# Attention with beacon keys followed by an ELU feed-forward layer: moving the ELU's second half from VectorE to ScalarE, and issuing the attention casts whole

## The chip, the cores and the metric

The kernel runs on one core of one Trainium2 chip. The metric is the device time of one execution in microseconds. The profiled span is 1.6 to 1.9 us shorter than the device time, because the profile counts from the first to the last instruction.

Engine names: PE is TensorE (matrix multiply; PEld is its weight load), DVE is VectorE, ACT is ScalarE, POOL is GpSimd, SP is SyncE. "Two-input" means an elementwise instruction that reads two tensors.

## The reference, cut to what matters

```python
# attention over 8 batches, 8 heads, 576 queries, 16 beacon keys in front of 576 causal keys, D = 64
scores = scale * np.matmul(q, k_all.transpose(0, 1, 3, 2))
scores = np.where(causal, -1e9, scores)
a = np.exp(scores - scores.max(-1, keepdims=True)); a /= a.sum(-1, keepdims=True) + 1e-09
x = (a @ v_all)                            # -> 4608 tokens x 512
# feed-forward
h = x @ w_in                               # 512 -> 2048
g = np.where(h > 0.0, h, np.exp(np.minimum(h, 0.0)) - 1.0)      # ELU
return g @ w_out                           # 2048 -> 512
```

## The kernel before

The program is one hand-ordered list of steps. The list fixes the order of each engine's own instructions, and in the timelines below DVE takes its instructions in that order: at one place of the changed kernel it sat idle for 0.54 us while the inputs of `M` became ready, and still ran the two instructions emitted ahead of `M` first. The 4608 tokens are cut into output tiles of 512 (the first one into two halves, numbered 0 and 1). A **stage** is one tile of the feed-forward layer together with one attention batch: stages 2 to 7 have both, stages 8 and 9 have no attention left. A stage has 16 **chunks**; a chunk is one block of 128 hidden units for 512 tokens, and between its own matmuls it carries a slice of the previous tile's output projection and of the attention.

The steps that the argument touches:

```python
@step
def F(t, i):     # PE: hidden matmul, four 128-deep matmuls into PSUM bank hps (two such banks)
@step
def e(t, i):     # ACT: e = exp(h), PSUM -> SBUF fp32
    eb[t, i] = melt.tile([P, 512], FP32, tag="e", bufs=2, name="e")
    nc.scalar.activation(out=eb[t, i], in_=flat(hp[t, i]), func=AFT.Exp, bias=0.0, scale=1.0)
@step
def r(t, i):     # DVE: r = min(e, 1) - 1, SBUF -> SBUF
    rb[t, i] = melt.tile([P, 512], FP16, tag="r", name="r")
    nc.vector.tensor_scalar(
        out=rb[t, i], in0=eb[t, i], scalar1=1.0, scalar2=1.0, op0=ALU.min, op1=ALU.subtract)
@step
def g(t, i):     # DVE: g = max(h, r); reads PSUM, so it is what frees the hps bank
    ...
    nc.vector.tensor_tensor(out=gh[k][:, i % UN, :], in0=flat(hp[t, i]), in1=rb[t, i], op=ALU.max)
```

`S` is a score matmul (into one of the PSUM banks that scores, row sums and attention outputs share), `x` its Exp on ACT, `m` the causal mask product on DVE. `L` and `W` are the matmuls for row sums and attention output, `n` the reciprocal on ACT, and `M` the product on DVE that writes the attention output into `xT` and thereby frees its PSUM bank. `Q` and `J` are the output projection and its eviction; it uses Strassen's scheme, for which `Z` makes sums of `gt` on DVE and `wt` makes sums of the weights, once.

The attention inputs of later batches are cast from fp32 to bf16 by DMAs that POOL issues. Before, each cast of q or k is cut into four pieces (the five loads of the values are issued one by one), and in front of each, from tile 2 on, POOL makes a one-element copy of the newest hidden chunk (a **gate**), so that the issue falls at a known place relative to DVE's work (in front of the 57 gates POOL waited 70.3 us in sum for DVE's `gt`):

```python
def gated():
    if last[0] is not None and last[0][0] >= 2:
        nc.gpsimd.tensor_copy(out=gate, in_=gh[...][0:1, last[0][1] % UN, 0:1])
@step
def kq(b, c):                        # one of 8 pieces: two heads of q or of k
    ...
    gated()
    nc.gpsimd.dma_start(out=scr[b, n_][:, hs, :], in_=(q, k)[n_][b, hs].rearrange("h s d -> s h d"))
```

The softmax here doesn't subtract the row's maximum and nothing guards it: scores larger than these inputs give would overflow.

## Time and profile before

The median was 359.14 us in three runs (358.25 to 359.36).

| | before |
|---|---|
| profiled span | 356.5 us |
| PE, DVE, ACT, POOL busy | 95%, 81%, 65%, 38% |
| stages 2 to 8, start to start | 33.37, 39.71, 37.81, 37.56, 36.67, 35.56, 26.37 us |

Stage lengths here and below are computed from the trace as the time from the first hidden matmul of a stage to that of the next. (The prediction writes 39.1 us for stage 3; the trace gives 39.71, and the prediction's 3.0 us above stage 6 fits that figure.) The busy line of the profile page, and the start of its chain (the work that ended last, followed back), of the kernel before:

```profile
PE 339.9 (95%) x4331; PEld 209.3 (59%) x4331; DVE 290.5 (81%) x655; ACT 233.4 (65%) x363; POOL 136.1 (38%) x207
PE 63%; DVE 24%; ACT 8%; issue 3%; ACTq 0%; DVEq 0%
```

PE is the fullest engine, and a quarter of the chain runs through DVE. The groups of instructions of the same kernel (line, engine, operation, output<-inputs, count | busy us, mean ns of one | idle time of the engine just before them, and what ended it):

```profile
L438 PE MATMUL hps<-xT,w_in 128*128 128x512 f16 (+1 forms) x640 | 147.8, 359 | 5.6 <-DVE gt L462 5.4
L448 ACT ACTIVATE e<-hps 128x512 f32<-128x512 f32 x144 | 86.1, 599 | 54.3 <-PE hps L438 52.8
L462 DVE TENSOR_TENSOR gt<-hps,r 128x512 f16<-128x512 f32 x144 | 99.5, 691 | 6.1
L453 DVE TENSOR_SCALAR r<-e 128x512 f16<-128x512 f32 x144 | 72.2, 501 | 12.7 <-ACT e L448 11.1
L568 POOL COPY gate<-gt 1x1 f16<-1x1 f16 x57 | 18.5, 324 | 70.5 <-DVE gt L462 70.3
L583 POOL DMA_DIRECT2D scr<-in_q_dram x20 | 27.3, 1365 | 2.0 <-DMA w_out<-in_moe_w_out_dram 1.5
```

ELU takes two DVE passes, `r` (501 ns on average) and `g` (691 ns), 1.19 us of DVE per chunk, while ACT idles 54 us in front of its Exps. The mean of `r` hides two populations: the 91 that no POOL cast touches take 421 ns, and the 53 that stand beside a cast take 638 ns on average and up to 1.29 us. The waits of PE, with their totals, number and longest, in us:

```profile
PE hps L438 <- DVE gt L462: 5.4, 13, 0.8
PE sc L279 <- DVE xT L386: 2.3, 4, 0.9
PE sc L279 <- ACT et L289: 1.1, 3, 0.7
PE ut L316 <- issue: 1.0, 1, 1.0
```

The first line is the one the change aims at: PE wants the hidden bank, and DVE's `g` has not yet freed it. Here is one at the end of stage 4:

```profile
176.15 0.49 DVE L406 TENSOR_TENSOR xT<-ut,rl 128x128 f16<-128x128 f32 x2 [0.74 <-ACT rl L352]
...
177.10 0.69 DVE L462 TENSOR_TENSOR gt<-hps,r 128x512 f16<-128x512 f32 x1
...
177.84 1.02 PE L438 MATMUL hps<-xT,w_in 128*128 128x512 f16 x4 [0.52 <-DVE gt L462]
```

The `g` that frees the bank stood behind the last `M` of the stage (L406), which had itself waited for the reciprocal on ACT.

### The profile page before, as it was taken

The numbers are of one execution on the slowest core, as the hardware profiler recorded it, in microseconds if no ns is written. First come the engines' busy times: TensorE is split into PE (matmuls) and PEld (weight loads), VectorE is DVE, ScalarE is ACT, GpSimd is POOL, SyncE is SP. The second block draws the span as 40 slices with busy tenths as digits, with TensorE's granted clock in tenths as the row PEclk, the third lists the DMA queues.
The fourth block names the chain that finished last, engine by engine and source line by source line (L and its number), as shares of the span: only waits on it lengthen the run. The fifth ranks groups of instructions, "written<-read, shape, count | busy, mean of one in ns | idle before, by whom it ended". The sixth has DMA issues, their size and how long they took to land.

```text
span 356.5 us, 10381 instructions
## 1 busy us (share of the span) xinstructions
PE 339.9 (95%) x4331; PEld 209.3 (59%) x4331; DVE 290.5 (81%) x655; ACT 233.4 (65%) x363; POOL 136.1 (38%) x207
## 2 busy tenths in 40 slices
...
GB/s 121 159 191 185 180 204 145 122 174 80 127 94 112 102 107 73 155 104 99 63 163 104 95 94 110 152 5 31 61 32 2 31 59 32 29 61 30 31 88 90
DMA packets 127759, 34.76 MB, mean 98 GB/s; under 512 B 111328, under 2 KB 126176, under 8 KB 127712
## 3 DMA queue, kind: packets, MB, share of 16 engines
...
q10 hardware_dynamic: 576, 0.13, 0.2%
...
## 4 chain that ended last, share of the span: by engine, by line
PE 63%; DVE 24%; ACT 8%; issue 3%; ACTq 0%; DVEq 0%
PE hps L438 25%; PE ops L535 18%; DVE gt L462 6%; PE sc L279 5%; DVE r L453 5%; PE lt L316 5%; ACT et L289 3%; PE ops L471 3%; DVE xT L386 3%; DVE gt L492 3%; DVE osb L551 2%; PE ut L316 2%; PE w L206 2%; DVE et L305 2%; ACT rl L349 2%
## 5 line engine op out<-in xcount | busy, mean ns | idle before, releaser
L438 PE MATMUL hps<-xT,w_in 128*128 128x512 f16 (+1 forms) x640 | 147.8, 359 | 5.6 <-DVE gt L462 5.4
L448 ACT ACTIVATE e<-hps 128x512 f32<-128x512 f32 x144 | 86.1, 599 | 54.3 <-PE hps L438 52.8
L289 ACT ACTIVATE et<-sc 128x832 f16<-128x832 f32 x128 | 104.3, 871 | 16.3 <-PE sc L279 15.0
L462 DVE TENSOR_TENSOR gt<-hps,r 128x512 f16<-128x512 f32 x144 | 99.5, 691 | 6.1
L535 PEld LDWEIGHTS <-gt 128*128 128x128 f16 x768 | 75.2, 98 | 28.8
L438 PEld LDWEIGHTS <-w_in 128*128 128x128 f16 x640 | 56.7, 97 | 52.7 <-issue 13.5
L453 DVE TENSOR_SCALAR r<-e 128x512 f16<-128x512 f32 x144 | 72.2, 501 | 12.7 <-ACT e L448 11.1
L535 PE MATMUL ops<-wt,gt 128*128 128x256 f16 x384 | 52.5, 273 | 0.0
L535 PE MATMUL ops<-w_out,gt 128*128 128x256 f16 x384 | 51.4, 273 | 0.0
L305 DVE TENSOR_TENSOR et<-et,triu 128x256 f16<-128x256 f16 (+2 forms) x164 | 38.5, 268 | 13.7 <-ACT et L289 13.3
L568 POOL COPY gate<-gt 1x1 f16<-1x1 f16 x57 | 18.5, 324 | 70.5 <-DVE gt L462 70.3
L134 POOL DMA_DIRECT2D v<-in_v_dram x40 | 34.4, 865 | 7.8 <-issue 3.5
L492 DVE TENSOR_TENSOR gt<-gt 128x1024 f16<-128x1024 f16 x48 | 32.5, 681 | 0.0
L583 POOL DMA_DIRECT2D scr<-in_q_dram x20 | 27.3, 1365 | 2.0 <-DMA w_out<-in_moe_w_out_dram 1.5
L583 POOL DMA_DIRECT2D scr<-in_k_dram x20 | 27.2, 1361 | 1.2 <-DMA w_out<-in_moe_w_out_dram 1.2
L316 PEld LDWEIGHTS <-v 128*32 128x32 f16 x1248 | 20.7, 94 | 9.6 <-issue 3.5
L279 PE MATMUL sc<-qkd 64*128 64x208 bf16 (+5 forms) x320 | 22.3, 252 | 2.4 <-DVE xT L386 2.3
L551 DVE TENSOR_TENSOR osb<-ops,sm 128x512 f32<-128x512 f32 x24 | 16.4, 681 | 4.4 <-issue 3.4
L279 PEld LDWEIGHTS <-qkd 64*128 64x128 bf16 x320 | 11.2, 94 | 14.0 <-issue 9.3
L316 PE MATMUL ut<-et,v 128*32 128x64 f16 (+6 forms) x840 | 17.0, 225 | 1.4 <-issue 1.0
L544 ACT COPY sm<-ops 128x512 f32<-128x512 f32 x24 | 14.3, 595 | 5.3 <-PE ops L535 5.2
L535 PE MATMUL ops<-w_out,s 128*128 128x256 f16 x128 | 17.6, 273 | 0.0
...
## 6 DMA issues: line engine op xcount, KB each, us to landing
...
```

Source lines behind the costliest of these rows:

```text
L134: nc.gpsimd.dma_start(out=st[b][2][r0:r0 + n, j, :, :], in_=v[b, :, ilo[j]:ilo[j] + n, :].rearrange("h s d -> s h d"),)
L279: nc.tensor.matmul(out=s[:, h, a - c0:e - c0], lhsT=t[D * h:D * (h + 1), 1, P * j:P * (j + 1)], rhs=t[D * h:D * (h + 1), 0, NB + qa + a - ...
L289: nc.scalar.activation(out=ets[b, p][:, :, GW * g:GW * (g + 1)], in_=sc[b, p, g][:, :, 0:GW], func=AFT.Exp, bias=0.0, scale=SCALE)
L305: nc.vector.tensor_tensor(out=o, in0=o, in1=triu[0:kc[j], :, t0:t0 + e - a], op=ALU.mult)
L316: nc.tensor.matmul(out=t[32 * i:32 * (i + 1), a - qa:e - qa], lhsT=ones[0:kc[j], :] if half is None else v16[0:kc[j], j, h, 32 * half:32 * ...
L438: nc.tensor.matmul(out=h[:, n_, :], lhsT=w_in16[:, cc, P * fc:P * (fc + 1)], rhs=xt[k][:, cc, a - TT * k:e - TT * k], start=(cc == 0), sto ...
L448: nc.scalar.activation(out=eb[t, i], in_=flat(hp[t, i]), func=AFT.Exp, bias=0.0, scale=1.0)
L453: nc.vector.tensor_scalar(out=rb[t, i], in0=eb[t, i], scalar1=1.0, scalar2=1.0, op0=ALU.min, op1=ALU.subtract)
L462: nc.vector.tensor_tensor(out=gh[k][:, i % UN, :], in0=flat(hp[t, i]), in1=rb[t, i], op=ALU.max)
L492: nc.vector.tensor_tensor(out=o_, in0=a_, in1=b_, op=op_)
L535: nc.tensor.matmul(out=xy[t, n_][:, qd, :], lhsT=lw[:, P * qd:P * (qd + 1)], rhs=wt_[:, c, :], start=(first and qd == 0 and c == 0), stop= ...
L583: nc.gpsimd.dma_start(out=scr[b, n_][:, hs, :], in_=(q, k)[n_][b, hs].rearrange("h s d -> s h d"))
```

## The change

The intent: ELU(h) = min(exp(h) - 1, relu(h)). (For h > 0 exp(h) - 1 is the larger, for h < 0 relu is 0 and exp(h) - 1 is below it.) From the last four chunks of tile 1 on (132 of the 144 chunks of the kernel), both Exp and Relu leave PSUM on ACT, and DVE joins them in one pass that touches only SBUF. That gives DVE one pass per chunk in place of two, and the hidden PSUM bank is freed by ACT. With `r` gone from there on, the casts are no longer cut up nor gated. The diff, cut to its core:

```diff
     def e(t, i):
-        eb[t, i] = melt.tile([P, 512], FP32, tag="e", bufs=2, name="e")
+        eb[t, i] = melt.tile([P, 512], FP32, tag="e", bufs=3, name="e")
         nc.scalar.activation(out=eb[t, i], in_=flat(hp[t, i]), func=AFT.Exp, bias=0.0, scale=1.0)
+    @step
+    def u(t, i):
+        rb[t, i] = melt.tile([P, 512], FP16, tag="r", name="r")
+        nc.scalar.activation(out=rb[t, i], in_=flat(hp[t, i]), func=AFT.Relu, bias=0.0, scale=1.0)
+    @step
+    def kk(t, i):
+        nc.vector.scalar_tensor_tensor(
+            out=half(t, i), in0=eb[t, i], scalar=1.0, in1=rb[t, i], op0=ALU.subtract, op1=ALU.min)
+    op["k"] = kk
...
-    def gated():
-        if last[0] is not None and last[0][0] >= 2:
-            nc.gpsimd.tensor_copy(out=gate, in_=gh[...][0:1, last[0][1] % UN, 0:1])
...
-        gated()
-        hs = slice(2 * x_, 2 * x_ + 2)
-        nc.gpsimd.dma_start(out=scr[b, n_][:, hs, :], in_=(q, k)[n_][b, hs].rearrange("h s d -> s h d"))
+        t = scr[b, n_] = dram.tile([S, H, D], BF16, tag=f"scr{n_}", name="scr")
+        nc.gpsimd.dma_start(out=t[:, :, :], in_=(q, k)[n_][b].rearrange("h s d -> s h d"))
... (in the lists: r.t.i g.t.i become u.t.i k.t.i; lv.c.0 to lv.c.4 become lv.c; eight kq become lk.d.0 lk.d.1)
```

The order of PE's 4331 matrix multiplies is the same before and after.

More of the change, by code (lines that the diff above doesn't have):

```diff
@@ L446, in e, with half @@
     def e(t, i):
-        eb[t, i] = melt.tile([P, 512], FP32, tag="e", bufs=2, name="e")
+        eb[t, i] = melt.tile([P, 512], FP32, tag="e", bufs=3, name="e")
         nc.scalar.activation(out=eb[t, i], in_=flat(hp[t, i]), func=AFT.Exp, bias=0.0, scale=1.0)
+    @step
+    def u(t, i):
+        rb[t, i] = melt.tile([P, 512], FP16, tag="r", name="r")
+        nc.scalar.activation(out=rb[t, i], in_=flat(hp[t, i]), func=AFT.Relu, bias=0.0, scale=1.0)
+    def half(t, i):
+        k = t, i // UN
+        if k not in gh:
+            gh[k] = gpool.tile([P, UN, 512], FP16, tag="g", name="gt")
+        return gh[k][:, i % UN, :]
+    @step
[3 more added lines that the diff above has]
+    op["k"] = kk
     @step
@@ L457, in g @@
     def g(t, i):
-        k = t, i // UN
-        if k not in gh:
-            gh[k] = gpool.tile([P, UN, 512], FP16, tag="g", name="gt")
-        last[0] = t, i
-        nc.vector.tensor_tensor(out=gh[k][:, i % UN, :], in0=flat(hp[t, i]), in1=rb[t, i], op=ALU.max)
+        nc.vector.tensor_tensor(out=half(t, i), in0=flat(hp[t, i]), in1=rb[t, i], op=ALU.max)
     @step
@@ L561, with lk @@
     scr, qkd = {}, {}
-    last = [None]
-    gate = konst.tile([1, 1], FP16, name="gate")
-    def gated():
-        if last[0] is not None and last[0][0] >= 2:
-            nc.gpsimd.tensor_copy(out=gate, in_=gh[last[0][0], last[0][1] // UN][0:1, last[0][1] % UN, 0:1])
-    @step
-    def lk(b):
-        new_stage(b)
-        load_qk(b, 0, H)
-    @step
-    def kq(b, c):
-        x_, n_ = c // 2 % 2 + 2 * (c // 4), c % 2
-        if c < 2:
-            scr[b, n_] = dram.tile([S, H, D], BF16, tag=f"scr{n_}", name="scr")
-        gated()
-        hs = slice(2 * x_, 2 * x_ + 2)
-        nc.gpsimd.dma_start(
-            out=scr[b, n_][:, hs, :], in_=(q, k)[n_][b, hs].rearrange("h s d -> s h d"))
+    @step
+    def lk(b, n_=None):
+        if b < BD:
+            new_stage(b)
+            load_qk(b, 0, H)
+            return
+        t = scr[b, n_] = dram.tile([S, H, D], BF16, tag=f"scr{n_}", name="scr")
+        nc.gpsimd.dma_start(out=t[:, :, :], in_=(q, k)[n_][b].rearrange("h s d -> s h d"))
     @step
@@ L601, in lv @@
     @step
-    def lv(b, *js):
-        gated()
-        load_v(b, list(js) or list(range(NKC)))
+    def lv(b):
+        load_v(b, list(range(NKC)))
     def run(names):
@@ L613 @@
     run("""
-    warm.12 bt bk cb.0.0 cb.0.1 cb.0.3 cb.0.2 warm.3 T.0.0 ck.0.0 cq.0.0 warm.4.64 S.0.0.0 S.0.0.1
-    T.0.1 x.0.0.0 cq.0.1 m.0.0.0 x.0.0.1 S.0.0.2 warm.1.64 S.0.0.3 ck.0.1 x.0.0.2 cb.1.0 warm.1.64
-    T.0.2 S.0.1.0 x.0.0.3 x.0.1.0 warm.1.64 S.0.1.1 m.0.0.2 cq.0.2 x.0.1.1 warm.2.64 S.0.1.2
-    warm.2.64 T.0.3 wo.0 wo.1 lv.1 lk.2 wo.2 wo.3 m.0.0.3 x.0.1.2 S.0.1.3 ck.0.2 m.0.1.0 m.0.1.2
-    ck.0.3 warm.5.64 S.0.3.0 x.0.1.3 warm.2.64 S.0.2.0 cb.1.1 x.0.3.0 m.0.1.3 x.0.2.0 m.0.3.0
@@ L619 @@
-    warm.2.64 S.0.3.1 warm.2.64 S.0.2.1 x.0.3.1 m.0.2.0 x.0.2.1 warm.2.64 S.0.3.2 x.0.3.2 L.0.A
-    S.0.3.3 n.0.A x.0.3.3 cb.1.3 m.0.3.2 W.0.A.1 T.1.0 M.0.A.1 m.0.3.3 W.0.A.0 S.0.2.2 W.0.B.0.1
-    ck.1.0 M.0.A.0 x.0.2.2 S.0.2.3 cb.1.2 T.1.1 x.0.2.3 m.0.2.2 S.1.0.0 ck.1.1 m.0.2.3 F.0.0 e.0.0
-    r.0.0 F.0.3 x.1.0.0 g.0.0 m.1.0.0 W.0.B.1.1 e.0.3 S.1.0.1 S.1.1.0 x.1.0.1 F.0.2 r.0.3 x.1.1.0
-    e.0.2 g.0.3 L.0.B m.1.0.1 m.1.1.0 n.0.B S.1.1.1 F.0.1 r.0.2 g.0.2 F.0.5 M.0.B.0.1 M.0.B.1.1
-    x.1.1.1 S.1.1.2 S.1.0.2 W.0.B.0.0 m.1.1.1 e.0.1 r.0.1 x.1.1.2 e.0.5 W.0.B.1.0 lv.2 g.0.1 x.1.0.2
@@ L625 @@
-    M.0.B.0.0 S.1.0.3 F.0.7 x.1.0.3 e.0.7 cb.2.0 T.1.2 r.0.5 m.1.1.2 m.1.0.2 ck.1.2 T.1.3 g.0.5
-    m.1.0.3 r.0.7 F.0.4 ck.1.3 g.0.7 e.0.4 M.0.B.1.0 S.1.1.3 F.0.6 cb.2.1 x.1.1.3 G.0.0.0 r.0.4 kq.3.0
-    g.0.4 e.0.6 m.1.1.3 r.0.6 kq.3.1 S.1.3.0 S.1.3.1 x.1.3.1 g.0.6 F.1.1 m.1.3.1 e.1.1 x.1.3.0 G.0.1.0
-    F.1.0 r.1.1 kq.3.2 g.1.1 S.1.3.2 e.1.0 m.1.3.0 r.1.0 kq.3.3 x.1.3.2 S.1.2.0 x.1.2.0 F.1.2 G.0.0.1 g.1.0 e.1.2
-    S.1.3.3 S.1.2.1 m.1.3.2 F.1.5 m.1.2.0 x.1.3.3 cb.2.2 x.1.2.1 r.1.2 kq.3.4 S.1.2.2 e.1.5 g.1.2 F.1.3
@@ L630 @@
-    m.1.3.3 G.0.1.1 x.1.2.2 m.1.2.1 r.1.5 kq.3.5 e.1.3 g.1.5 m.1.2.2 S.1.2.3 r.1.3 kq.3.6 T.2.0 x.1.2.3 ck.2.0
-    g.1.3 F.1.6 F.1.7 S.2.0.0 S.2.0.1 e.1.6 x.2.0.0 x.2.0.1 G.0.0.2 S.2.0.2 m.1.2.3 x.2.0.2
-    G.0.1.2 T.2.1 r.1.6 kq.3.7 g.1.6 e.1.7 m.2.0.0 T.2.2 m.2.0.1 ck.2.1 m.2.0.2 G.0.0.3 ck.2.2 L.1.0 r.1.7
-    W.1.0.0 g.1.7 S.2.0.3 o.0.0 n.1.0 cb.2.3 F.1.4 M.1.0.0 x.2.0.3 e.1.4 m.2.0.3 G.0.1.3 r.1.4
-    W.1.0.1 o.0.1 L.1.1 M.1.0.1 g.1.4 W.1.1.0 n.1.1 W.1.1.1 M.1.1.0 R.1 S.2.1.0 M.1.1.1 x.2.1.0
@@ L635 @@
-    G.1.1.0 n.1.R m.2.1.0 M.1.R F.2.1 F.2.0 e.2.1 S.2.1.1 S.2.1.2 e.2.0 r.2.1 g.2.1 G.1.1.1 r.2.0
-    F.2.2 x.2.1.1 S.2.2.0 x.2.1.2 S.2.2.1 g.2.0 m.2.1.1 e.2.2 F.2.3 x.2.2.0 m.2.1.2 x.2.2.1 r.2.2
-    G.1.0.0 e.2.3 g.2.2 lv.3.0 m.2.2.0 m.2.2.1 r.2.3 F.2.4 S.2.2.2 g.2.3 lv.3.1 e.2.4 S.2.1.3 x.2.2.2 r.2.4
-    g.2.4 lv.3.2 G.1.1.2 F.2.5 m.2.2.2 lt.3 x.2.1.3 m.2.1.3 e.2.5 T.2.3 ck.2.3 F.2.6 r.2.5 G.1.1.3
-    g.2.5 lv.3.3 e.2.6 S.2.2.3 S.2.3.0 F.2.8 o.1.1 x.2.2.3 G.1.0.1 r.2.6 x.2.3.0 S.2.3.1 m.2.2.3
@@ L640 @@
-    L.2.0 e.2.8 x.2.3.1 W.2.0.0 g.2.6 lv.3.4 W.2.0.1 m.2.3.0 s.0.0 r.2.8 g.2.8 kq.4.0 s.0.1 m.2.3.1 F.2.7 wt.1.0 n.2.0
-    M.2.0.1 e.2.7 M.2.0.0 F.2.9 wt.1.1 S.3.0.0 e.2.9 S.2.3.2 G.1.0.2 r.2.7 g.2.7 kq.4.1 x.3.0.0 x.2.3.2
-    F.2.11 wt.2.0 S.3.0.1 e.2.11 x.3.0.1 r.2.9 m.3.0.0 g.2.9 kq.4.2 m.2.3.2 r.2.11 g.2.11 kq.4.3 s.1.1 S.2.3.3 m.3.0.1
-    F.2.10 wt.2.1 x.2.3.3 G.1.0.3 e.2.10 S.3.0.2 m.2.3.3 o.1.0 x.3.0.2 S.3.0.3 F.2.12 wt.4.0 r.2.10 m.3.0.2 g.2.10 kq.4.4
-    L.2.1 e.2.12 W.2.1.0 x.3.0.3 s.1.0 r.2.12 F.2.14 wt.4.1 g.2.12 kq.4.5 Z.2.3.0 m.3.0.3 n.2.1 M.2.1.0 F.2.13 e.2.14
@@ L645 @@
-    W.2.1.1 e.2.13 r.2.14 R.2 g.2.14 kq.4.6 Z.2.1.0 r.2.13 F.2.15 g.2.13 kq.4.7 M.2.1.1 n.2.R M.2.R
-    e.2.15 r.2.15 g.2.15 Z.2.3.1
-    """)
-    def SC(b, p, g0):
-        if b < B:
-            for g_ in (g0, g0 + 1):
-                run(f"S.{b}.{p}.{g_} x.{b}.{p}.{g_} m.{b}.{p}.{g_}")
-    def LW(b, g):
-        run(f"L.{b}.{g} W.{b}.{g}.0 n.{b}.{g} M.{b}.{g}.0")
-    def WR(b, g):
-        run(f"W.{b}.{g}.1" + g * f" R.{b}" + f" M.{b}.{g}.1" + g * f" n.{b}.R M.{b}.R")
-    SLOTS = [0, 1, 2, 4, 5, 6, 7, 8, 9, 11, 12, 13]
@@ L661 @@
-    NQ = 14 * NPR // NFC
-    SUMS = {0: [(-1, 1, 1)], 2: [(-1, 2, 0)], 3: [(-1, 2, 1)], 5: [(-1, 4, 0)], 6: [(-1, 4, 1)],
-            11: [(0, 3, 0)], 12: [(0, 1, 0)], 15: [(0, 3, 1)]}
-    for b in range(3, NT // TT + 2):
-        todo = {}
-        if b < B:
-            todo = dict(zip(SLOTS, [
-                lambda: SC(b, 1, 0), lambda: SC(b, 1, 2), lambda: LW(b, 0),
-                lambda: SC(b, 2, 0), lambda: SC(b, 2, 2), lambda: WR(b, 0),
-                lambda: SC(b, 3, 0), lambda: SC(b, 3, 2), lambda: LW(b, 1),
-                lambda: SC(b + 1, 0, 0), lambda: SC(b + 1, 0, 2), lambda: WR(b, 1)]))
+    warm.12 bt bk cb.0.0 cb.0.1 cb.0.3 cb.0.2 warm.3 T.0.0 ck.0.0 cq.0.0 warm.4.64 S.0.0.0
@@ new lines @@
+    S.0.0.1 T.0.1 x.0.0.0 cq.0.1 m.0.0.0 x.0.0.1 S.0.0.2 warm.1.64 S.0.0.3 ck.0.1 x.0.0.2 cb.1.0
+    warm.1.64 T.0.2 S.0.1.0 x.0.0.3 x.0.1.0 warm.1.64 S.0.1.1 m.0.0.2 cq.0.2 x.0.1.1 warm.2.64
+    S.0.1.2 warm.2.64 T.0.3 wo.0 wo.1 lv.1 lk.2 wo.2 wo.3 m.0.0.3 x.0.1.2 S.0.1.3 ck.0.2 m.0.1.0
+    m.0.1.2 ck.0.3 warm.5.64 S.0.3.0 x.0.1.3 warm.2.64 S.0.2.0 cb.1.1 x.0.3.0 m.0.1.3 x.0.2.0
+    m.0.3.0 warm.2.64 S.0.3.1 warm.2.64 S.0.2.1 x.0.3.1 m.0.2.0 x.0.2.1 warm.2.64 S.0.3.2
+    x.0.3.2 L.0.A S.0.3.3 n.0.A x.0.3.3 cb.1.3 m.0.3.2 W.0.A.1 T.1.0 M.0.A.1 m.0.3.3 W.0.A.0
@@ new lines @@
+    S.0.2.2 W.0.B.0.1 ck.1.0 M.0.A.0 x.0.2.2 S.0.2.3 cb.1.2 T.1.1 x.0.2.3 m.0.2.2 S.1.0.0 ck.1.1
+    m.0.2.3 F.0.0 e.0.0 r.0.0 F.0.3 x.1.0.0 g.0.0 m.1.0.0 W.0.B.1.1 e.0.3 S.1.0.1 S.1.1.0
+    x.1.0.1 F.0.2 r.0.3 x.1.1.0 e.0.2 g.0.3 L.0.B m.1.0.1 m.1.1.0 n.0.B S.1.1.1 F.0.1 r.0.2
+    g.0.2 F.0.5 M.0.B.0.1 M.0.B.1.1 x.1.1.1 S.1.1.2 S.1.0.2 W.0.B.0.0 m.1.1.1 e.0.1 r.0.1
+    x.1.1.2 e.0.5 W.0.B.1.0 lv.2 g.0.1 x.1.0.2 M.0.B.0.0 S.1.0.3 F.0.7 x.1.0.3 e.0.7 cb.2.0
+    T.1.2 r.0.5 m.1.1.2 m.1.0.2 ck.1.2 T.1.3 g.0.5 m.1.0.3 r.0.7 F.0.4 ck.1.3 g.0.7 e.0.4
@@ new lines @@
+    M.0.B.1.0 S.1.1.3 F.0.6 cb.2.1 x.1.1.3 G.0.0.0 lk.3.0 lk.3.1 r.0.4 g.0.4 e.0.6 m.1.1.3 r.0.6
+    S.1.3.0 S.1.3.1 x.1.3.1 g.0.6 F.1.1 m.1.3.1 e.1.1 x.1.3.0 G.0.1.0 F.1.0 r.1.1 g.1.1 S.1.3.2
+    e.1.0 m.1.3.0 r.1.0 x.1.3.2 S.1.2.0 x.1.2.0 F.1.2 G.0.0.1 g.1.0 e.1.2 S.1.3.3 S.1.2.1
+    m.1.3.2 F.1.5 m.1.2.0 x.1.3.3 cb.2.2 x.1.2.1 r.1.2 S.1.2.2 e.1.5 g.1.2 F.1.3 m.1.3.3 G.0.1.1
+    x.1.2.2 m.1.2.1 r.1.5 e.1.3 u.1.3 g.1.5 m.1.2.2 S.1.2.3 T.2.0 x.1.2.3 ck.2.0 k.1.3 F.1.6
+    F.1.7 S.2.0.0 S.2.0.1 e.1.6 u.1.6 x.2.0.0 x.2.0.1 G.0.0.2 S.2.0.2 m.1.2.3 x.2.0.2 G.0.1.2
@@ new lines @@
+    T.2.1 k.1.6 e.1.7 u.1.7 m.2.0.0 T.2.2 m.2.0.1 ck.2.1 m.2.0.2 G.0.0.3 ck.2.2 L.1.0 W.1.0.0
+    k.1.7 S.2.0.3 o.0.0 n.1.0 cb.2.3 F.1.4 M.1.0.0 x.2.0.3 e.1.4 u.1.4 m.2.0.3 G.0.1.3 W.1.0.1
+    o.0.1 L.1.1 M.1.0.1 k.1.4 W.1.1.0 n.1.1 W.1.1.1 M.1.1.0 R.1 S.2.1.0 M.1.1.1 x.2.1.0 G.1.1.0
+    n.1.R m.2.1.0 M.1.R F.2.1 F.2.0 e.2.1 u.2.1 S.2.1.1 S.2.1.2 e.2.0 u.2.0 k.2.1 G.1.1.1 F.2.2
+    x.2.1.1 S.2.2.0 x.2.1.2 S.2.2.1 k.2.0 m.2.1.1 e.2.2 u.2.2 F.2.3 x.2.2.0 m.2.1.2 x.2.2.1
+    G.1.0.0 e.2.3 u.2.3 k.2.2 m.2.2.0 m.2.2.1 F.2.4 S.2.2.2 k.2.3 e.2.4 u.2.4 S.2.1.3 x.2.2.2
@@ new lines @@
+    k.2.4 G.1.1.2 F.2.5 m.2.2.2 lt.3 x.2.1.3 m.2.1.3 e.2.5 u.2.5 T.2.3 ck.2.3 F.2.6 G.1.1.3
+    k.2.5 e.2.6 u.2.6 S.2.2.3 S.2.3.0 F.2.8 o.1.1 x.2.2.3 G.1.0.1 x.2.3.0 S.2.3.1 m.2.2.3 L.2.0
+    e.2.8 u.2.8 x.2.3.1 W.2.0.0 k.2.6 W.2.0.1 m.2.3.0 s.0.0 k.2.8 s.0.1 m.2.3.1 F.2.7 wt.1.0
+    n.2.0 M.2.0.1 e.2.7 u.2.7 M.2.0.0 F.2.9 wt.1.1 S.3.0.0 e.2.9 u.2.9 S.2.3.2 lv.3 G.1.0.2
+    k.2.7 x.3.0.0 x.2.3.2 F.2.11 wt.2.0 S.3.0.1 e.2.11 u.2.11 x.3.0.1 m.3.0.0 k.2.9 m.2.3.2
+    k.2.11 s.1.1 S.2.3.3 m.3.0.1 F.2.10 wt.2.1 x.2.3.3 G.1.0.3 e.2.10 u.2.10 S.3.0.2 m.2.3.3
@@ new lines @@
+    o.1.0 x.3.0.2 S.3.0.3 F.2.12 wt.4.0 m.3.0.2 k.2.10 L.2.1 e.2.12 u.2.12 W.2.1.0 x.3.0.3 s.1.0
+    lk.4.0 lk.4.1 F.2.14 wt.4.1 k.2.12 Z.2.3.0 m.3.0.3 n.2.1 M.2.1.0 F.2.13 e.2.14 u.2.14
+    W.2.1.1 e.2.13 u.2.13 R.2 k.2.14 Z.2.1.0 F.2.15 k.2.13 M.2.1.1 n.2.R M.2.R e.2.15 u.2.15
+    k.2.15 Z.2.3.1
+    """)
+    BODY = """
+    F.b.0 e.b.0 u.b.0 k.b.0 Q.z.0.7 Z.z.1.1 S.b.1.0 x.b.1.0 m.b.1.0 S.b.1.1 x.b.1.1 m.b.1.1
+    F.b.1 e.b.1 u.b.1 k.b.1 Q.z.7.14 S.b.1.2 x.b.1.2 m.b.1.2 S.b.1.3 x.b.1.3 m.b.1.3 lt.c F.b.2
```

39 lines of the change are left out of this document (20 added, 19 removed).

## The prediction

> **What bounds it now.** The page gives PE 95% busy, DVE 81%, ACT 65%, POOL 38%, span 356.5 us. In the timeline, stages 3 to 7 (16 hidden chunks, one attention batch and one output tile each) take 39.1, 37.8, 37.6, 36.7, 35.6 us; stages 8 and 9 (no attention) about 26. Those two run at 1.63 us per chunk, its matmuls back to back: PE alone. In stages 4 to 7 most chunks repeat to 0.01 us (2.56, 2.19, 2.89, 1.39 ...): PE-bound too. What is not PE: the waits view has PE waiting 13 times, 5.4 us, on DVE's max (gt, L462), nearly all between 83 and 107 us, where DVE also makes the weight sums; and single chunks of stages 3 to 5 run 0.7 us long. The chain puts 24% on DVE, which overstates it: DVE and PE are nearly in step.
>
> **What the change does.** PE's order is unchanged. Per chunk, from the groups view:
> - DVE loses TENSOR_SCALAR r (501 ns mean, 420 undisturbed) and the PSUM max (691), and gains one SBUF-only two-input pass, about 690 ns (estimate: the [...]rate of that max). 132 chunks: DVE busy falls by about 66 us, to near 225.
> - ACT gains a Relu, 599 ns by the Exp beside it, about 0.5 start to start: busy rises to about 312 us. Per attention stage ACT needs about 33 us start to start (estimate: 16 x 0.745 scores, 32 x 0.51, rest 5) against PE's 36.5; in stage 2 about 31.5, as much as PE: the tightest place.
> - The hidden PSUM bank is released by ACT's Relu, not after two passes in DVE's queue.
> - POOL loses 57 gates and has 10 whole casts for 40 pieces. In the trace r stretches to 0.9-1.29 us when POOL issues a cast, ending with it; two-input TENSOR_TENSORs (L305, L492) keep their time beside the same issues.[...] r is gone by the time casts flow, so large, ungated casts should cost nothing.[...]
>
> **On the critical path.** Matmul start-to-start time above the undisturbed pitch, with stage 6 as the floor, leaves removable: stage 2 2.8 us, stage 3 3.0, stage 4 1.1, stage 5 0.9, others near 0: 7.9 us at most, so 351.2 is the floor. I expect ACT to take back about 1 us in stage 2, and small losses elsewhere: a gain of 6.3 us from 66 us of DVE work saved.
>
> **Predicted: 352.8 us, 8 in 10 between 349.8 and 356.5.** Faster by over 2%: 0.33; within 2%: 0.63; slower by over 2%: 0.04.
>
> **Right or wrong by:** in the waits view, PE on DVE gt near zero; the new pass near 690 ns, not stretching beside POOL issues; stages 3 to 5 near 36.7 us, 8 and 9 unchanged; ACT near 88% and PE near 97% busy.
>
> **What would make it wrong:**[...] ACT lagging its two score banks in chunks with two Exp pairs (2.5 us of ACT against 2.2 of PE), giving PE waits on ACT; ungated bursts delaying transposes or output writes.

(Passages cut from it are marked. No term of the forecast's sum is cut: 359.1 us less the gain of 6.3 us is 352.8 us. That large casts should cost nothing was inference from the trace of the kernel before. Of the 53 passes of `r` beside a cast there, the 24 beside those of q or k averaged 803 ns, against 421 ns beside none. Of the two-input passes, 21 of L305 in the 128x256 form averaged 287 ns beside casts of q or k, against 285 ns beside none, and eight of L492 averaged 680 against 681 ns. That the new pass would behave like these, that trace did not show.)

## More of the kernel before

A difference under 2% is called "same" by the verdict, even when its 95% interval excludes 1; "unclear" is an interval that reaches across the 2% line. The kernel before itself ranged from 358.14 to 359.22 us in the medians of the four rounds of runs, so differences under about 1 us between experiments of different rounds mean little.

A stage from 3 on is emitted by a loop; its chunk 6, which matters later, comes out in this order (b this stage, z the one before): `F.b.6 e.b.6 r.b.6 g.b.6 (casts) Q.z.42.49 J.z.2 Z.z.4.1 W.b.0.1 M.b.0.1`, and then chunk 7 with `F.b.7 ... Q.z.49.56 S.b.3.0 x.b.3.0 m.b.3.0 S.b.3.1 ...`.

PE wants a score bank that DVE's `M` has not yet freed. Here is one instance of it, chunks 6 and 7 of stage 4, from the timeline of the kernel before (start us, duration us, engine, line, operation, output<-inputs, count, [idle before<-releaser]):

```profile
155.18 0.76 PE L316 MATMUL ut<-et,v 128*32 128x512 f16 x20
155.25 1.38 POOL L583 DMA_DIRECT2D scr<-in_q_dram  x1
155.70 1.15 DVE L453 TENSOR_SCALAR r<-e 128x512 f16<-128x512 f32 x1
156.89 0.69 DVE L462 TENSOR_TENSOR gt<-hps,r 128x512 f16<-128x512 f32 x1
157.50 0.68 DVE L492 TENSOR_TENSOR gt<-gt 128x1024 f16<-128x1024 f16 x1
...
158.09 0.75 DVE L386 TENSOR_TENSOR xT<-ut,rl 128x256 f16<-128x256 f32 x2
...
158.90 0.35 PE L279 MATMUL sc<-qkd 64*128 64x160 bf16 x4 [0.95 <-DVE xT L386]
```

Read it from the bottom. PE sat idle for 0.95 us until `M` (L386) was done. The attention matmuls that feed `M` (`ut`, from 155.18) had ended at 155.94 us, 2.15 us before `M` began; it stood in DVE's queue behind the sum `Z` (L492), behind `g`, behind an `r` that took 1.15 us beside a cast issue on POOL (421 ns on average with no such issue beside it).

## The result and the profile after

The changed kernel took 354.40 us (median of four, 354.02 to 354.90) against 359.22 us for the kernel before on the same chip. The ratio (computed as the mean time of one kernel's runs over that of the other's of the same rounds, so not quite the ratio of the medians that are quoted, here and below) is 0.9873, with a 95% interval of 0.9850 to 0.9895: 1.3% faster. Executions over 1.5% slower than the fastest of the same kernel are left out of the means. The outputs are right. A later repetition gave 354.02 against 358.14 us, ratio 0.988 (0.9865 to 0.9896).

> The changed kernel once more, unaltered, beside share_relu: 354.4 +- 0.7 us, ratio 0.987.

The busy line and the chain of the kernel after:

```profile
PE 339.2 (96%) x4331; PEld 210.1 (60%) x4331; DVE 232.9 (66%) x523; ACT 292.0 (83%) x495; POOL 86.6 (25%) x120
PE 70%; ACT 21%; DVE 6%; issue 2%; ACTq 0%
```

DVE lost 57.6 us of work and ACT took on 58.6 us; in the chain DVE's share became ACT's. The groups after:

```profile
L438 PE MATMUL hps<-xT,w_in 128*128 128x512 f16 (+1 forms) x640 | 147.6, 359 | 0.1
L463 DVE SCALAR_TENSOR_TENSOR gt<-e,r 128x512 f16<-128x512 f32 x132 | 91.3, 691 | 58.2 <-ACT r L453 57.5
L448 ACT ACTIVATE e<-hps 128x512 f32<-128x512 f32 x144 | 88.9, 617 | 21.5 <-PE hps L438 20.4
L453 ACT ACTIVATE r<-hps 128x512 f16<-128x512 f32 x132 | 81.9, 620 | 0.0
```

PE's idle time in front of the hidden matmuls is gone (5.6 to 0.1 us), as wanted. The new join takes 691 ns, the same as the old max. But DVE now waits 57.5 us for ACT's Relu in front of the joins: DVE has become a follower of ACT. PE's waits after:

```profile
PE ut L316 <- issue: 2.4, 2, 1.3
PE sc L279 <- ACT et L289: 1.9, 6, 0.7
PE sc L279 <- DVE xT L386: 1.8, 5, 0.4
```

`hps <- gt` has left the list; the wait for `M` has stayed (2.3 to 1.8 us, now once in each of five stages). Here is the same place of stage 4 as above, in the timeline after:

```profile
152.37 0.65 ACT L448 ACTIVATE e<-hps 128x512 f32<-128x512 f32 x1
152.42 0.76 PE L316 MATMUL ut<-et,v 128*32 128x512 f16 x20
152.85 0.67 ACT L453 ACTIVATE r<-hps 128x512 f16<-128x512 f32 x1
...
153.54 0.69 DVE L463 SCALAR_TENSOR_TENSOR gt<-e,r 128x512 f16<-128x512 f32 x1 [0.54 <-ACT r L453]
...
154.15 0.69 DVE L505 TENSOR_TENSOR gt<-gt 128x1024 f16<-128x1024 f16 x1
...
154.76 0.75 DVE L386 TENSOR_TENSOR xT<-ut,rl 128x256 f16<-128x256 f32 x2
...
155.56 0.35 PE L279 MATMUL sc<-qkd 64*128 64x160 bf16 x4 [0.37 <-DVE xT L386]
```

The matmuls that `M` needs (`ut`, from 152.42) were done around 153.2 us. DVE was idle for 0.54 us at that time, but the instruction at the head of its queue was the join, which waited for the Relu; `M` started 1.6 us later, at 154.76 us. Here an idle DVE did not let the ready `M` pass.

Where the time came from, stage by stage (us, computed from the traces):

```
stage      2      3      4      5      6      7      8
before  33.37  39.71  37.81  37.56  36.67  35.56  26.37
after   32.32  37.68  36.71  38.19  36.64  35.53  26.04
change  -1.05  -2.03  -1.10  +0.63  -0.03  -0.03  -0.33
```

Stage 9 gains another 0.32. Ahead of stage 2 the two kernels differ by 0.1 us in sum (0.6 us gained before any changed instruction runs, which is scatter of the start, and 0.7 us lost again between tile 1 and stage 2, where the trace has a 1.05 us pause of PE that is discussed below). The sum of all is the difference of the spans, 356.5 - 352.3 = 4.2 us.

Chunk lengths are sharper than stage lengths. Stage 4, chunks 0 to 15, computed likewise:

```
before  2.18 2.20 3.01 1.64 2.18 2.20 2.42 3.32 2.20 3.01 1.64 2.25 2.19 3.42 1.64 2.31
after   2.18 2.20 3.22 1.64 2.18 2.20 2.42 2.74 2.20 3.01 1.64 2.18 2.20 3.42 1.64 1.63
```

Chunks 7, 11 and 15 gained 0.58, 0.07 and 0.68 us, and chunk 2 lost 0.21. Chunk 7 is the one of the timelines above. It is 2.74 us after in every stage from 3 to 7, and was 2.58, 2.59 and 2.42 us in stages 5, 6 and 7 before: in these three stages the change made it longer. In stage 6, which the prediction took as the floor, chunk 7 lost 0.15, chunk 2 lost 0.15, and chunk 15 gained 0.33.

Chunk 15 is where most of the gain of the later stages lies: 0.69, 0.69, 0.03, 0.33 and 0.50 us in stages 3 to 7, 2.2 us in all. PE no longer waits there for `g` to free the hidden bank. Experiment 8 tests this.

### The profile page after: what moved, and what is told of

It is laid out like the page before. It is cut to its first block, busy times and chain, and to the rows that moved or that the text cites. A ratio compares the mean times of both kernels' runs of the same rounds, so it can differ in the third digit from the quotient of the medians.

```text
span 352.3 us, 10230 instructions
## 1 busy us (share of the span) xinstructions
PE 339.2 (96%) x4331; PEld 210.1 (60%) x4331; DVE 232.9 (66%) x523; ACT 292.0 (83%) x495; POOL 86.6 (25%) x120
## 4 chain that ended last, share of the span: by engine, by line
PE 70%; ACT 21%; DVE 6%; issue 2%; ACTq 0%
PE hps L438 29%; PE ops L548 23%; ACT et L289 11%; PE lt L316 5%; PE sc L279 5%; ACT r L453 4%; ACT e L448 3%; PE ut L316 3%; DVE gt L463 3%; PE ops L484 2%; PE w L206 2%; DVE xT L386 1%; ACT qk L258 1%; DVE gt L505 1%; PE ub L316 1%
## 5 line engine op out<-in xcount | busy, mean ns | idle before, releaser
L463 DVE SCALAR_TENSOR_TENSOR gt<-e,r 128x512 f16<-128x512 f32 x132 | 91.3, 691 | 58.2 <-ACT r L453 57.5
L289 ACT ACTIVATE et<-sc 128x832 f16<-128x832 f32 x128 | 106.3, 902 | 2.4 <-PE sc L279 2.3
L448 ACT ACTIVATE e<-hps 128x512 f32<-128x512 f32 x144 | 88.9, 617 | 21.5 <-PE hps L438 20.4
L453 ACT ACTIVATE r<-hps 128x512 f16<-128x512 f32 x132 | 81.9, 620 | 0.0
L305 DVE TENSOR_TENSOR et<-et,triu 128x256 f16<-128x256 f16 (+2 forms) x164 | 40.7, 272 | 20.5 <-ACT et L289 17.7
L129 POOL DMA_DIRECT2D v<-in_beacon_v_dram x8 | 4.3, 540 | 66.5 <-PE ut L316 58.6
L557 ACT COPY sm<-ops 128x512 f32<-128x512 f32 x24 | 15.2, 634 | 5.0 <-PE ops L548 5.0
L386 DVE TENSOR_TENSOR xT<-lt,rl 128x448 f16<-128x448 f32 (+6 forms) x28 | 10.6, 419 | 11.2 <-ACT rl L352 11.2
L279 PE MATMUL sc<-qk 64*128 64x208 bf16 (+11 forms) x208 | 15.4, 245 | 2.0 <-ACT et L289 1.5
```

The costliest lines, as they stand in the source:

```text
L279: nc.tensor.matmul(out=s[:, h, a - c0:e - c0], lhsT=t[D * h:D * (h + 1), 1, P * j:P * (j + 1)], rhs=t[D * h:D * (h + 1), 0, NB + qa + a - ...
L289: nc.scalar.activation(out=ets[b, p][:, :, GW * g:GW * (g + 1)], in_=sc[b, p, g][:, :, 0:GW], func=AFT.Exp, bias=0.0, scale=SCALE)
L305: nc.vector.tensor_tensor(out=o, in0=o, in1=triu[0:kc[j], :, t0:t0 + e - a], op=ALU.mult)
L453: nc.scalar.activation(out=rb[t, i], in_=flat(hp[t, i]), func=AFT.Relu, bias=0.0, scale=1.0)
L463: nc.vector.scalar_tensor_tensor(out=half(t, i), in0=eb[t, i], scalar=1.0, in1=rb[t, i], op0=ALU.subtract, op1=ALU.min)
```

## The experiments

The expectations quoted below speak of a theory 1 (and a variant 1a) and a theory 2. To read them: **theory 1** is the account of the prediction. The gain is ELU's, from taking DVE out of PE's way; what is left is PE's own work, with ACT's small losses; the casts without gates cost nothing and bring nothing; and in its variant 1a, the DVE time that is now free is of no use, so filling it would cost nearly nothing. The rival to its first half is that the uncut casts bring part of the gain or take part of it back. **Theory 2** came from the timelines above: a part of the loss is still there, and it is a matter of order in DVE's queue. `M` stands behind the ELU's passes: behind `r` and `g` before, behind a join that waits for ACT after. Nine more kernels were run, and the changed kernel once more.

### 1. The new ELU with the old casts (elu_only)

The changed kernel, with the cut-up and gated casts put back:

```diff
-        nc.gpsimd.dma_start(out=t[:, :, :], in_=(q, k)[n_][b].rearrange("h s d -> s h d"))
+        gated()
+        hs = slice(2 * x_, 2 * x_ + 2)
+        nc.gpsimd.dma_start(
+            out=scr[b, n_][:, hs, :], in_=(q, k)[n_][b, hs].rearrange("h s d -> s h d"))
... (and lv, kq where they stood before)
```

> The new ELU with the old, gated, cut-up casts. Theory 1 (the gain is the ELU's: no r for POOL to block, PSUM freed by ScalarE, VectorE lighter): all of the gain stays, 354.4 +- 0.7 us, and the 0.6 us steps at chunk 8 of stages 3 and 4 are gone. Rival (the whole, ungated casts bring a good part): 356 to 358 us.

Measured: 353.80 us (353.56 to 354.31) against 359.15, ratio 0.9853 (0.9825 to 0.9881). The interval overlaps that of the changed kernel (0.9850 to 0.9895). The whole gain is ELU's. Chunk 7 of stages 3 and 4 (the text of the expectation counts it as the eighth) fell from 3.3 to 2.74 us, as expected. Removing 57 gates and 30 cast pieces took 51 us of busy time from POOL (137.4 to 86.6) and moved the kernel's time by nothing that can be measured.

### 2. The old ELU with whole, ungated casts (casts_only)

The kernel before, with the casts of the change:

```diff
-        gated()
-        hs = slice(2 * x_, 2 * x_ + 2)
-        nc.gpsimd.dma_start(
-            out=scr[b, n_][:, hs, :], in_=(q, k)[n_][b, hs].rearrange("h s d -> s h d"))
+        t = scr[b, n_] = dram.tile([S, H, D], BF16, tag=f"scr{n_}", name="scr")
+        nc.gpsimd.dma_start(out=t[:, :, :], in_=(q, k)[n_][b].rearrange("h s d -> s h d"))
```

> The old ELU (r and max on VectorE) with whole, ungated casts. Theory 1[...]: r waits for casts of 2.2 us and value loads of 0.9 us back to back, up to about 2 us at a time, in stages 2 to 5; slower than before by 0.5 to 3 us (360 to 362). Rival (ungated casts are a gain in themselves): 356 to 358 us.

Measured: 366.99 us (365.26 to 370.17), ratio 1.0233 (1.0190 to 1.0276), "unclear" by the verdict but slower beyond the noise. The direction was expected, the size was not: 7.8 us slower than before. The timeline of casts_only (of an execution of 369.36 us) shows why:

```profile
71.71 2.23 POOL L577 DMA_DIRECT2D scr<-in_q_dram  x1
...
72.19 4.22 DVE L453 TENSOR_SCALAR r<-e 128x512 f16<-128x512 f32 x1 [0.49 <-ACT e L448]
...
73.41 2.75 POOL L577 DMA_DIRECT2D scr<-in_k_dram  x1
...
77.19 1.86 PE L438 MATMUL hps<-xT,w_in 128*128 128x512 f16 x4 [3.37 <-DVE gt L462]
```

One `r`, 0.42 us when left alone, lasted 4.22 us: from 0.5 us into the issue of the q cast until 0.25 us after that of the k cast. Two issues that overlap (2.23 and 2.75 us) thus held one such pass through both. (POOL takes 2.30 us to issue the whole cast of q and 2.61 us that of k on average in this run, 2.25 and 2.66 us in the changed kernel; a cut-up piece before took 1.36 us.) The second line to read is the last: PE waited 3.37 us, and then its four matmuls took 1.86 us, where they take 1.04 elsewhere. The granted clock of these 10 us (70 to 80) was 0.80, of the next 10 it was 0.86, and between 110 and 120, around a second such hold with a wait of 3.79 us, it was 0.68; in the changed kernel all three are 1.00. The windows of casts_only (stretch, its length, busy us of PE, PEld, DVE, ACT and POOL with their instructions, granted clock, DMA share, GB/s):

```profile
70.00:80.00 10.00, 6.63 (x37) 2.57 (x35) 8.27 (x12) 4.88 (x8) 6.16 (x4) 0.80 1.96 192
110.00:120.00 10.00, 6.21 (x55) 3.29 (x56) 9.65 (x15) 3.44 (x6) 4.94 (x4) 0.68 2.10 134
```

The matmuls after the first wait show it too: groups of four 128x512 matmuls took 1.86, 1.89 and 1.71 us at 77.2, 79.8 and 81.5 us, and 1.04 us again at 83.75. So this one long hold was paid twice, as a wait and as slow matmuls after it. That the wait is what slowed them was not tested; the run shows the two together at these two places. Over whole executions the granted clock of casts_only was 0.979 to 0.995, that of the kernel before in the same round 0.998 to 1.000.

In the changed kernel the same casts do nothing to the join, which reads two tensors. From the timeline after:

```profile
71.00 2.25 POOL L583 DMA_DIRECT2D scr<-in_q_dram  x1
72.70 2.77 POOL L583 DMA_DIRECT2D scr<-in_k_dram  x1
72.71 0.69 DVE L463 SCALAR_TENSOR_TENSOR gt<-e,r 128x512 f16<-128x512 f32 x1 [0.69 <-ACT r L453]
```

The join that stands wholly inside the two issues takes its 0.69 us. Over all 132 joins, the 22 beside POOL's DMA issues and the 110 away from them both average 691 ns. So the new ELU is what permits the simpler casts, and the casts themselves bring nothing that can be measured.

### 3. DVE load put back (dve_load)

The changed kernel, with a useless pass behind each join, which added 0.46 us of busy time each (60.2 us for 132; of SBUF data only, so that the hidden bank's release stays where it is). The sum goes to `e`, which nobody reads again:

```diff
             out=half(t, i), in0=eb[t, i], scalar=1.0, in1=rb[t, i], op0=ALU.subtract, op1=ALU.min)
+        o_ = eb[t, i][:, 0:360]
+        nc.vector.tensor_tensor(out=o_, in0=o_, in1=rb[t, i][:, 0:360], op=ALU.add)
```

> The changed kernel with an idle VectorE pass of about 0.45 us behind each join, so that VectorE is as busy as before (about 290 us). The result is still right. Theory 1a (what pays is that the PSUM bank no longer waits for VectorE's queue): 354.4 to 355.2 us. Rival 1b (VectorE's own load was the limit in stages 2 and 3): back to 357 us or more.

Measured: 365.87 us (365.04 to 366.27), ratio 1.0186 (1.0159 to 1.0213), "unclear" by the verdict but slower beyond the noise. Variant 1a fell. The load brings DVE to 293.1 us busy, much like before (290.5), and costs 11.5 us against the changed kernel: DVE, with 34% of its time free, has no slack where it counts. The loss is not even: stage 2 kept its 32.35 us, while stage 3, which also has weight sums on DVE, took 42.61 us in place of 37.68. The time is even longer than before's, perhaps because ACT has more to do as well (292.1 us busy, 233.4 before). The added pass also holds the buffers of `e` and `r` for longer. Neither was tested. PE's waits in dve_load:

```profile
PE sc L279 <- DVE xT L386: 4.7, 5, 0.9
PE hps L438 <- DVE xT L386: 2.0, 1, 2.0
```

Both top waits are for `M`, in DVE's queue, now behind a longer row. This is what led from theory 1 to theory 2.

### 4. Without the Relu (no_relu)

ACT's Relu is left out, and the join reads `e` twice: min(e - 1, e) = e - 1. This is wrong for h > 0, but it passed the tolerance, since h is small here. It also leaves the Exp as the only reader of the hidden bank (PE waited for that bank once in this run, 0.2 us). It is a floor, not a version.

```diff
     def u(t, i):
-        rb[t, i] = melt.tile([P, 512], FP16, tag="r", name="r")
-        nc.scalar.activation(out=rb[t, i], in_=flat(hp[t, i]), func=AFT.Relu, bias=0.0, scale=1.0)
+        pass
...
-            out=half(t, i), in0=eb[t, i], scalar=1.0, in1=rb[t, i], op0=ALU.subtract, op1=ALU.min)
+            out=half(t, i), in0=eb[t, i], scalar=1.0, in1=eb[t, i], op0=ALU.subtract, op1=ALU.min)
```

> Wrong result on purpose: no Relu on ScalarE, the join reads e twice, so ScalarE carries its old load and VectorE the new one. Gives the floor that the Relu keeps us from. Theory (ScalarE took back 1.7 us between 59 and 95 us and a few tenths in stages 4 to 7): 352 to 352.9 us. Rival (PE alone is the limit, the missing gain is elsewhere): 354 us or more.

Measured: 347.70 us (347.05 to 349.55), ratio 0.9688 (0.9661 to 0.9716). The expectation missed by over 4 us, and this is the most telling miss: with PE's work and order unchanged, the kernel ran 3.5 us below the 351.2 us that the prediction called the floor. Stage by stage:

```
stage      2      3      4      5      6      7      8
after   32.32  37.68  36.71  38.19  36.64  35.53  26.04
no_relu 30.44  36.41  35.95  37.03  35.95  34.81  26.04
```

Stage 6 can be done in 35.95 us; before took 36.67. In stage 4 of no_relu, chunk 2 took 3.01 us, chunk 7 2.19 and chunk 15 1.63. The changed kernel (3.22, 2.74, 1.63) and the kernel before (3.01, 3.32, 2.31) differ from it there and hardly anywhere else in this stage. So the Relu on ACT costs 6.7 us against a DVE join that needs none (354.4 - 347.7), although ACT is free for 17% of the time. By place, the profiled spans differ by 7.0 us: 1.9 in stage 2, 2.7 in the five chunks 7, 0.8 in the chunks 2 of stages 4 to 7, 0.7 in chunks 0 and 1 of stage 3, and 0.9 in the start and in a pause that is discussed below. How much of this is ACT's load and how much ACT's lateness was not separated.

### 5. `M` ahead of the join (hoist_m)

The test of theory 2. In stages 3 to 7 the join and the sum of chunk 6 are emitted behind `W` and `M`. Nothing is added or taken away:

```diff
-    ... F.b.6 e.b.6 u.b.6 k.b.6 Q.z.42.49 J.z.2 Z.z.4.1 W.b.0.1 M.b.0.1 F.b.7 ...
+    ... F.b.6 e.b.6 u.b.6 Q.z.42.49 J.z.2 W.b.0.1 M.b.0.1 k.b.6 Z.z.4.1 F.b.7 ...
```

> The changed kernel with one thing moved: in chunk 6 of stages 3 to 7 the join and the Strassen sum stand behind the attention multiply M in VectorE's queue, not in front of it. Theory 2 (PE waits in chunk 7 for a score bank that M frees, and M waits in VectorE's queue behind a join that waits for ScalarE's Relu): chunk 7 falls from 2.74 to 2.2 us in five stages, the kernel by 2.5 to 2.8 us to about 351.8. Rival (ScalarE's extra half microsecond per chunk binds through the score banks themselves, whatever VectorE's order): less than 0.7 us.

Measured: 351.83 us (351.39 to 353.84), against 358.43 for before, ratio 0.9819 (0.9789 to 0.9848), "unclear" by the verdict, since the interval crosses the 2% line. That is 2.6 us below the changed kernel by the medians and 2.5 us by the profiled spans. Chunk 7 became 2.19 us in all five stages (it was 2.74), which is five times 0.55 us; about 0.07 us per stage came back in chunk 9. The same place in stage 4, in the timeline of hoist_m:

```profile
152.06 0.76 PE L316 MATMUL ut<-et,v 128*32 128x512 f16 x20
...
152.89 0.76 DVE L386 TENSOR_TENSOR xT<-ut,rl 128x256 f16<-128x256 f32 x2 [0.25 <-PE ut L316]
...
153.56 0.68 DVE L463 SCALAR_TENSOR_TENSOR gt<-e,r 128x512 f16<-128x512 f32 x1
...
154.48 0.53 PE L279 MATMUL sc<-qkd 64*128 64x416 bf16 x6
```

`M` now waits only for its matmuls and fills DVE's idle gap; the join starts 1.50 us after the `ut` matmuls did, in place of 1.12 us, and that holds nobody up. PE runs all six score matmuls in one go, with no wait. The wait `sc <- xT` has gone from PE's list. Theory 2 holds for chunk 7.

### 6. A wider reordering (reorder)

The same idea everywhere: in chunks with scores, Relu and join are emitted behind the Exps and masks; the last `M` of stage 2 is put ahead of a join; the last weight sums come later.

```diff
-    F.b.0 e.b.0 u.b.0 k.b.0 Q.z.0.7 Z.z.1.1 S.b.1.0 x.b.1.0 m.b.1.0 S.b.1.1 x.b.1.1 m.b.1.1
+    F.b.0 e.b.0 Q.z.0.7 Z.z.1.1 S.b.1.0 x.b.1.0 m.b.1.0 S.b.1.1 x.b.1.1 m.b.1.1 u.b.0 k.b.0
... (likewise in chunks 1, 4, 5, 7, 8, 11 and 12; chunk 6 as in hoist_m)
```

> hoist_m, and in the chunks with score pairs the Relu and the join behind the pair's Exps and mask products; M before the join at the end of stage 2; the last weight sum three chunks later in stage 3. No work is removed. Theory 2: chunk 2 falls from 3.2 to 3.0 us in stages 4 to 7, and stage 3 loses its stalls of 0.2 and 0.6 us in chunks 0 and 1: 350 to 350.8 us. Rival (ScalarE's total load binds): no faster than hoist_m.

Measured: 352.74 us (352.14 to 352.93), ratio 0.9831 (0.9804 to 0.9858). The expectation missed: it is not faster than hoist_m. Chunk 1 of stage 3 lost its stall (2.20 us, 2.78 in hoist_m), but chunk 2 of stages 4 to 7 took 3.16 us where 3.0 was expected, chunk 5 of stage 3 grew to 2.61 us (2.20), and chunk 15 grew to 1.98 us in stages 3, 4 and 6 (1.63). PE's pause in stage 5 was 1.7 us this time. At the end of those three chunks 15 PE waited 0.19 us for ACT's Relu, and ACT in stage 4 had waited 2.08 us for the last `M`s on DVE. That these `M`s were late because the joins, now later, stand in front of them is argued, not shown.

### 7. The old kernel with `M` ahead (before_hoist)

If theory 2 is right, the loss was in the kernel before too, and can be had there without the change. In chunk 6 of stages 3 to 7, `r` and `g` are emitted behind `M`:

```diff
-                run(f"F.{b}.{i} e.{b}.{i} r.{b}.{i} g.{b}.{i}")
+                run(f"F.{b}.{i} e.{b}.{i}")
+                if i != 6:
+                    run(f"r.{b}.{i} g.{b}.{i}")
... (for i == 6: todo[6](), which has W and M, then r g, then the casts, then Z)
```

> The kernel before, with r and max of chunk 6 behind M in stages 3 to 7; nothing of the change is in it. Theory 2: chunk 7 falls from 3.3 to 2.2-2.4 us in stages 3 and 4, from 2.6 to 2.2 in 5 and 6: 2.5 to 3.2 us, about 356.3. If theory 2 is wrong, or the cast that blocks r keeps chunk 7 long all the same: 358.5 us or more.

Measured: 355.82 us (median of five runs, 355.48 to 356.64; a sixth, at 361.01 us, was slow), ratio 0.9924 (0.9899 to 0.9950). Chunk 7 became 2.19 to 2.20 us (from as much as 3.32), while PE's wait for `gt` stayed (5.8 us, 13 times). A part came back elsewhere: chunk 9 of stages 3 and 4 took 3.28 us in place of 3.01. So about 2.6 of the 358.4 us of this round were a matter of order alone, with the reservation that two cast pieces and the sum of the chunk were moved along; and stages 5 to 7 before were no floor.

### 8. The bank released late (late_free)

How much of the gain is the earlier release of the hidden bank? In the changed kernel, DVE reads one column of the bank behind each join, so that ACT's Relu no longer frees it:

```diff
             out=half(t, i), in0=eb[t, i], scalar=1.0, in1=rb[t, i], op0=ALU.subtract, op1=ALU.min)
+        nc.vector.tensor_copy(out=tiny, in_=flat(hp[t, i])[:, 0:1])
```

> The changed kernel with a one-column VectorE read of the hidden bank behind each join, so the bank is freed by VectorE's queue again; VectorE's load grows by some 0.07 us per chunk. Theory 1a (the early release is what pays in stages 2 and 3): PE waits on this read in stage 2 and at the start of stage 3, 1.5 to 4 us lost, 356 to 358. Rival (release place does not matter, the load of the queue does): under 355.3 us.

Measured: 357.00 us (356.30 to 358.48), ratio 0.9959 (0.9932 to 0.9986). PE's waits in late_free:

```profile
PE hps L439 <- DVE tiny L466: 2.5, 5, 0.6
PE sc L279 <- DVE xT L386: 2.2, 5, 0.4
```

More than half of the gain is gone, and the wait for the hidden bank is back. By place, 2.5 of the 3.0 us by which the profiled span is longer than the changed kernel's lie in chunk 15 of stages 3 to 7. In stage 4 this chunk took 2.35 us, against 1.63 after and 2.31 before, and PE waits at its end for the tiny read:

```profile
175.72 1.04 PE L439 MATMUL hps<-xT,w_in 128*128 128x512 f16 x4 [0.56 <-DVE tiny L466]
```

So the early release is what won chunk 15. The tiny reads also add 7.5 us of DVE work (240.4 against 232.9 us busy, 0.057 us for each of the 132), whose part was not separated; dve_load, with eight times as much work added, brought this chunk to 2.08 us only.

### 9. Both engines share the Relu (share_relu)

A version built from what the runs showed: hoist_m, with 13 of the 132 Relus on DVE, in the places where ACT is late (most of stage 2, chunk 1 of each later attention stage), and the last weight sums spread over chunks 3 and 6 of stage 3.

```diff
+    ON_DVE = {(1, 6), (1, 7), (2, 0), (2, 2), (2, 4), (2, 6), (2, 9), (3, 0)} | {(t, 1) for t in range(3, 8)}
...
         rb[t, i] = melt.tile([P, 512], FP16, tag="r", name="r")
+        if (t, i) in ON_DVE:
+            nc.vector.tensor_scalar(
+                out=rb[t, i], in0=flat(hp[t, i]), scalar1=0.0, scalar2=0.0, op0=ALU.max, op1=ALU.add)
+            return
```

> hoist_m with 13 of the 132 Relus given back to VectorE (from PSUM[...]): 2 in tile 1, 5 in tile 2, and in stages 3 to 7 that of chunk 1 (and chunk 0 of stage 3); the last weight sums spread over chunks 3 and 6 of stage 3. Theory (in tile 1 and stage 2 ScalarE's total load is what binds, and in chunk 2 of later stages its lag of half a microsecond): stage 2 falls from 32.2 to about 31.3 us, chunk 2 to 3.0, stage 3 to about 36.5: 349.8 to 351 us. Rival (every pass added to VectorE's queue costs PE more than ScalarE's relief brings, as dve_load and reorder showed): 351.8 us or more.

Measured: 349.79 us (349.40 to 350.10), against 358.14 for before, ratio 0.9758 (0.9743 to 0.9773): the best correct kernel, and faster than both kernels given. The groups of share_relu:

```profile
L455 DVE TENSOR_SCALAR r<-hps 128x512 f16<-128x512 f32 x13 | 9.0, 689 | 6.3 <-ACT e L449 6.2
L468 DVE SCALAR_TENSOR_TENSOR gt<-e,r 128x512 f16<-128x512 f32 x132 | 91.1, 691 | 46.7 <-ACT r L458 45.4
```

A Relu on DVE took 689 ns on average, one on ACT 610 ns. DVE's wait for Relus fell from 57.5 to 45.4 us. Stage 2 went from 32.2 us in hoist_m to 31.31, and chunk 2 is back at 3.01 us in stages 4 to 7. The one miss is stage 3, which was expected near 36.5 us and took 37.18: its chunk 2 took 4.04 us (3.47 in hoist_m). PE waited 0.49 us there for a mask product, which stood in DVE's queue behind two of the Relus given back and their joins: at this place the rival held. What the Relus and what the weight sums contributed was not separated.

### What stays open

PE has pauses of 0.5 to 1.7 us in front of an attention matmul for which the waits view gives "issue", that is, no semaphore that the profile shows. The kernel before has one at 211.99 us, in chunk 13 of stage 5; the changed kernel has one at 65.21 and one at 208.57 us. Every trace has the one in stage 5: chunk 13 took between 4.50 (no_relu) and 5.28 us (reorder) there, against 3.42 in the other stages. In all twelve traces a 16 KB packet of the instruction queue (q8 in the page) ended 1.25 to 1.55 us before PE went on. That PE waited for its own instructions is thus possible, but it rests on this coincidence alone: before and after have 34 such packets each, and no more than two have a pause beside them. The pause near 65 us is in the nine kernels with whole casts and in none of the three with cut-up casts (before, elu_only, before_hoist); why was not tested. It stands where 0.7 us are lost ahead of stage 2, and the longer one makes 0.29 us of the 0.63 us by which stage 5 got longer; the rest of stage 5 is chunks 2 and 7 (0.21 and 0.15). The pause varies from run to run: in after_again stage 5 took 37.83 us.

## Why the prediction was right or wrong, point by point

The time was well inside the range: 354.4 us measured, 352.8 predicted, 349.8 to 356.5 as the range, and "within 2%" as the likeliest class (0.63). The gain was 4.8 us in place of 6.3.

- **"PE on DVE gt near zero"**: right. 5.4 us before, not on the list after.
- **"the new pass near 690 ns, not stretching beside POOL issues"**: right, 691 ns in both cases. The new join, 128x512 from an fp32 and an fp16 source, takes as long as the old max (691 ns), from which the prediction had its figure.
- **"large, ungated casts should cost nothing"**: right (elu_only against the changed kernel), and casts_only shows that it holds only because `r` is gone.
- **ACT near 88% and PE near 97% busy**: ACT 83%, PE 96%. The 312 us for ACT is the old 233 plus 132 Relus at 599 ns each. But a Relu starts 0.48 us after the Exp in front of it, while both records last over 0.6 us; so each added only 0.44 us of busy time, and the total is 292 us.
- **"stages 3 to 5 near 36.7 us, 8 and 9 unchanged"**: 37.68, 36.71 and 38.19. Right for stage 4; stages 8 and 9 gained 0.3 us each.
- **"I expect ACT to take back about 1 us in stage 2"**: right in kind. Stage 2 gained 1.05 us where 1.8 was expected (2.8 removable less 1), so ACT took back more than expected. ACT was busy 30.75 of the 33.0 us from 66.4 to 99.4.

The step that failed is **"Matmul start-to-start time above the undisturbed pitch, with stage 6 as the floor ... so 351.2 is the floor"**. It failed in two ways. First, stage 6 was taken as pure PE because it was the best of its kind and its chunks repeat to 0.01 us. But a wait that recurs in every stage at the same place repeats just as exactly. Stage 6 held 0.40 us in chunk 7, in which PE waited for `M` in DVE's queue, and 0.33 us in chunk 15, in which PE waited for `g`, behind the last `M` (chunks 2.59 and 1.96, against 2.19 and 1.63 in no_relu), and no_relu ran it in 35.95 us, not 36.67. The waits view had both lines: `sc <- xT`, 2.3 us, and `hps <- gt`, of which the prediction put nearly all between 83 and 107 us, though a third lies outside. Second, the "0.9" of stage 5 was counted as DVE's to give back. It was the one "issue" pause: chunk 13 took 4.62 us in stage 5 against 3.42 in stage 6, which is 1.20 us, less 0.30 us that chunk 15 was shorter. No kernel returned it (4.50 us at the least), and stage 5 got 0.63 us longer instead.

The two errors have opposite signs, so a part of the good agreement of the total is luck. More could be gained than the sum said (no_relu, share_relu), and less of it was gained than the sum expected. What the Relu takes back goes two ways. In chunk 7 of five stages the join, waiting for the Relu, put about 0.5 us of idle DVE in front of `M`: 2.7 us in all against no_relu, and hoist_m gets them back. The prediction did not have this way. In stage 2, in chunks 0 and 1 of stage 3 and in chunks 2 of stages 4 to 7 (1.9, 0.7 and 0.8 us against no_relu) it is more nearly what its warning says, "ACT lagging its two score banks in chunks with two Exp pairs". PE's waits in stages 2 and 3 name ACT's score Exp (0.4 us in front of `sc`, `lt` and `ut` each), and in chunk 2 of stage 4 DVE's mask product waited 0.46 us for that Exp, and PE's row sums behind it ran 0.2 us longer.

The tacit step behind "a gain of 6.3 us from 66 us of DVE work saved" was that most of DVE's freed time was slack. dve_load speaks against it (60 us put back cost 11.5 us), and hoist_m shows that the order in the queue counts beside the load (2.6 us from the order alone).
